# A limit of three outstanding loads on the input stream of a decay attention with gated convolution (Trainium2, one core)

## The chip, the cores and the metric

The kernel runs on one core of a Trainium2 chip (trn2). The metric is device time in microseconds (us), lower is better. The time before is a median of 216.62 us over three runs (216.39 to 217.88).

## The reference

Two stages. The first is a blocked linear attention with a decay `lam` per head: 4 batches, 8 heads, 768 positions, head size 64, in 12 blocks of 64 positions that carry a state from one block to the next. The second takes its output as x (4 x 768 x 512), makes a gate out of a causal convolution of 5 taps per channel, and two products with 512 x 512 weights.

```python
for b in range(nb):                                    # 12 blocks of 64
    qb, kb, vb = (q[:, :, sl], k[:, :, sl], v[:, :, sl])
    intra = einsum('bhij,bhjd->bhid', einsum('bhic,bhjc->bhij', qb, kb) * Dmask, vb)
    inter = einsum('bhid,bhde->bhie', qb * lam_pow, kv_state)
    out[:, :, sl] = intra + inter
    kv_state = lam_block * kv_state + einsum('bhsd,bhse->bhde', kb * rev_pow, vb)
# x = out with the heads side by side
gate = sigmoid(causal_conv5(x, conv_w))
return (gate * (x @ w_val)) @ w_out
```

## The kernel before

The work is cut into 12 steps, i = 0 to 11, one for each block of 64 positions of all batches and heads. In a step TensorE makes the scores (L469), the outer product for the state (L500), the products of scores and v (`cross` and `own`, both L535) and the part that comes from the state (`inter`, L548). The result x goes on to the convolution, whose taps run on VectorE (L659), to the product with `w_val` (`value`, L722) and, times the gate, to the product with `w_out` (`project`, L789). Both weights, and the taps, are split into a high and a low part, so that each of these products is made of three.

The order of all this is written out by hand, in the list `ORDER` (L39 to L90): 12 steps overlap, and each entry emits its instructions on its engine in turn. Every engine works through its own instructions in that order and waits where an operand isn't there; an entry that comes late holds up all behind it on the same engine.

Loads are entries of the same list. A step has one buffer `ld` (128 x 4 x 2 x 512 float32, three in rotation), filled by eight transfers of 128 x 512 (256 KB): four for q and k with the head dimension on the partitions (`ld5-q0` for step 5), two for v (`ld5-v`) and two for k with positions on the partitions (`ld5-k`). All loads and all stores of the output are issued on SyncE's queue (L333, L800), one after the other; if one has to wait, those behind it wait too. A load into a buffer waits until TensorE, ScalarE and GpSimd have read what lay there. Each transfer also carries one of eight semaphores in turn (`DMAHW0` to `DMAHW7`), and the next transfer with the same one is issued only once the former has landed: no more than eight are on their way at a time.

Who needs what: `scores` (L469) takes all four q and k pieces of its step; its first 32 products need the first two, its last 32 the other two. GpSimd scales q (L446) out of the first and third piece. `cross` needs both pieces of v, and `scale_k` (L426 on ScalarE, L430 on GpSimd) the two of k.

The lines of `land` in `plan_load` that the change touches:

```python
for part, w in where:
    nc.sync.dma_start(lds[i]["all"][:, part, w], qkv[i][:, part, w])
```

Of the kernel before, what the change touches and what calls it, by code (L numbers as in the profile page):

```python
# [31 lines left out]
H_DVE = ()  # L32
U_SPLIT = ()
T_POOL = ((5, 3),)

OVER = {"DVE": 60, "ACT": 85, "POOL": 45}

# [62 lines left out]
class Plan:  # L100
# [5 lines left out]
    def add(self, engine, ns, fn, after=(), bufs=(), lag=60, mode=0, port=False, many=0, kind=None, name=None):  # L106

        kind = kind or fn.__name__
        n = self.kinds[kind] = self.kinds.get(kind, -1) + 1
        self.names.append(name or f"{kind}{n}")  # L110
        for b in bufs:
            b.users += 1
        over = OVER.get(engine, 0)
        self.work.append(
            (engine, ns - over, fn, [a for a in after if a is not None], list(bufs), 0.0, lag + over, mode, port, many)
        )
        return len(self.work) - 1
# [20 lines left out]
def decay_attention_then_gated_conv(  # L138
# [9 lines left out]
    nc = tc.nc  # L148
# [16 lines left out]
    def buf(tag, name, shape, dt=F32):  # L165
        return work.tile(shape, dt, name=name, tag=tag, bufs=SLOTS[tag])
# [145 lines left out]
        return [t_hi, on("DVE", 1060, low, [t_hi]) if low_dve else on("POOL", 2250, low, [t_hi])]  # L312


    lds = {}
    t_ld, ld_buf = {}, {}

    def plan_load(i):
        ld_buf[i] = Buf("ld")

        def land(where, i=i):
            if i not in lds:
                t = buf("ld", "ld", [P, 4, 2, DM])
                hd = t.rearrange("q p w (a b i) -> q p w a b i", a=2, b=NB)
                lds[i] = {
                    "all": t, "qT": hd[:, 0:2, 0], "kT": hd[:, 0:2, 1], "v": hd[:, 2:4, 0], "k": hd[:, 2:4, 1],
                }
            if i == 0 and len(set(part for part, _ in where)) == 1:
                part = where[0][0]
                nc.sync.dma_start(lds[i]["all"][:, part], qkv[i][:, part])  # L330
                return
            for part, w in where:
                nc.sync.dma_start(lds[i]["all"][:, part, w], qkv[i][:, part, w])  # L333

        both = ((0,), (1,)) if i < FINE else ((0, 1),)
        for parts in both:
            where = [(part, w) for part in parts for w in range(2)]
            t = add("DMA", 1400 * len(parts), lambda where=where, land=land: land(where), [], [ld_buf[i]], lag=2300,
                name=f"ld{i}-q{parts[0]}")
            for part in parts:  # L340
                t_ld[i, part] = t
        for w, what in enumerate("vk"):
            if w == 0 or i < N - 1:
                where = [(2, w), (3, w)]
                t_ld[i, what] = add("DMA", 1400, lambda where=where, land=land: land(where), [], [ld_buf[i]], lag=2300,
                name=f"ld{i}-{what}")
# [67 lines left out]
    for i in range(N):  # L414
# [218 lines left out]
        for ct in range(NT if split or j == UNIT - 1 else 0):  # L633
            where = "PE" if (un, ct) in T_PE else "POOL" if (un, ct) in T_POOL else "DVE"
            js, width = (slice(j, j + 1), L) if split else (slice(0, UNIT), UNIT * L)
# [217 lines left out]
```

## Time and profile before

| what | value |
|---|---|
| median of three runs | 216.62 us (216.39 to 217.88) |
| the profiled execution, its own time | 218.14 us |
| its span, first to last instruction | 216.4 us |
| TensorE busy | 199.0 us, 92% of the span |
| VectorE, ScalarE, GpSimd busy | 66%, 53%, 47% |
| moved by the DMA engines | 35.70 MB, mean 165 GB/s |
| stalls of TensorE that the chain shows after 45 us | 0.30, 1.62, 1.46 and 0.71 us |

The span holds the program's instructions alone; 1.7 us of the execution's time lie outside it. The profiled execution is 1.5 us over the median of the runs. Busy time is a mean over the whole span. What a wait costs is read from the chain that ended last, at the place where it stands.

### The profile page before, as it was taken

The numbers are of one execution on the slowest core, as the hardware profiler recorded it, in microseconds if no ns is written. First come the engines' busy times: TensorE is split into PE (matmuls) and PEld (weight loads), VectorE is DVE, ScalarE is ACT, GpSimd is POOL, SyncE is SP. The second block draws the span as 40 slices with busy tenths as digits, with TensorE's granted clock in tenths as the row PEclk, the third lists the DMA queues.
The fourth block names the chain that finished last, engine by engine and source line by source line (L and its number), as shares of the span: only waits on it lengthen the run. The fifth ranks groups of instructions, "written<-read, shape, count | busy, mean of one in ns | idle before, by whom it ended". The sixth has DMA issues, their size and how long they took to land.

```text
span 216.4 us, 8533 instructions
## 1 busy us (share of the span) xinstructions
PE 199.0 (92%) x3832; PEld 175.1 (81%) x3832; DVE 143.5 (66%) x220; ACT 114.1 (53%) x193; POOL 101.6 (47%) x81
## 2 busy tenths in 40 slices
PE   8838659999997899999799998999999999999993
PEld 3437659999986698798689988899889998899983
DVE  2998998999999649725923956919448832774100
ACT  3326876886853394237437642363741239855221
POOL 1171469155999209690409175018650052655600
PEclk9976978999999999999999999999999999999999
DMA  6999999157681396734155991612141001211022
GB/s 228 352 386 387 384 353 306 53 151 245 204 286 53 101 289 252 220 123 145 37 162 164 314 301 59 177 72 100 53 138 57 5 0 55 85 60 48 3 103 91
DMA packets 19188, 35.70 MB, mean 165 GB/s; under 512 B 2384, under 2 KB 2640, under 8 KB 19152
## 3 DMA queue, kind: packets, MB, share of 16 engines
q1 hardware_dynamic: 19008, 35.16, 47.9%
q8 instruction: 30, 0.49, 1.0%
q14 instruction: 6, 0.05, 0.1%
q10 hardware_dynamic: 144, 0.00, 0.0%
HBM read 28.86 MB, written 6.29 MB: 162 GB/s over the span
## 4 chain that ended last, share of the span: by engine, by line
PE 83%; DMA 7%; DVE 6%; issue 3%; SPq 1%; ACT 0%; DVEq 0%; ACTq 0%
PE op L789 32%; PE vp L722 31%; PE xp L535 5%; PE st L500 5%; PE xp L548 5%; PE s L469 4%; DMA w_raw<-in_w_out 3%; DMA w_raw<-in_w_val 2%; DMA lam_bc<-in_lam 2%; DVE w_m L276 1%; DVE w_e L267 1%; DVE w_m L250 1%; DVE w_m L283 1%; DVE w_e L244 1%; SPq L364 1%
## 5 line engine op out<-in xcount | busy, mean ns | idle before, releaser
L659 DVE SCALAR_TENSOR_TENSOR acc<-x,conv_sb,acc 128x512 f32<-128x512 f32 x92 | 69.3, 753 | 31.4 <-ACT acc L654 29.5
L789 PE MATMUL op<-wo_hi,hs 128*128 128x512 f32 (+1 forms) x200 | 61.2, 388 | 0.3 <-issue 0.3
L722 PE MATMUL vp<-x_hi,wv_hi 128*128 128x256 f32 x192 | 55.1, 287 | 0.0
L766 POOL TENSOR_TENSOR hs<-g,hs 128x512 fp32r<-128x512 f32 x24 | 31.4, 1326 | 48.8 <-ACT hs L763 48.8
L722 PE MATMUL vp<-x_lo,wv_hi 128*128 128x256 f32 x192 | 53.7, 280 | 0.0
L722 PE MATMUL vp<-x_hi,wv_lo 128*128 128x256 f32 x192 | 53.6, 279 | 0.0
L789 PEld LDWEIGHTS op<-wo_hi,hs 128*128 128x128 f32 x200 | 35.7, 188 | 7.2
L446 POOL TENSOR_TENSOR qd<-ld,qdec 128x512 f32<-128x512 f32 x22 | 29.0, 1335 | 24.9 <-DMA ld<-in_qkv 15.9
L789 PE MATMUL op<-wo_lo,hs 128*128 128x512 f32 (+1 forms) x100 | 38.4, 384 | 0.0
L722 PEld LDWEIGHTS vp<-x_hi,wv_hi 128*128 128x128 f32 x192 | 36.5, 190 | 1.3
L722 PEld LDWEIGHTS vp<-x_lo,wv_hi 128*128 128x128 f32 x192 | 36.4, 190 | 0.3
L722 PEld LDWEIGHTS vp<-x_hi,wv_lo 128*128 128x128 f32 x192 | 36.5, 190 | 0.0
L676 ACT ACTIVATE g<-acc 128x512 f32<-128x512 f32 x23 | 13.7, 598 | 29.3 <-DVE acc L659 29.3
L735 DVE TENSOR_TENSOR g<-vp,g 128x512 f32<-128x512 f32 x24 | 16.2, 687 | 18.1 <-ACT g L676 12.4
L797 ACT COPY o<-op 128x512 f32<-128x512 f32 (+1 forms) x25 | 14.0, 569 | 25.7 <-PE op L789 19.8
L617 POOL TENSOR_TENSOR x_lo<-x,x_hi 128x1024 fp32r<-128x1024 f32 x8 | 19.9, 2493 | 11.3 <-ACT x_hi L606 8.4
L789 PEld LDWEIGHTS op<-wo_lo,hs 128*128 128x128 f32 x100 | 18.8, 188 | 4.2 <-issue 0.5
L535 PE MATMUL xp<-A,ld 64*64 64x64 f32 x768 | 17.2, 228 | 4.9 <-issue 3.1
L535 PEld LDWEIGHTS xp<-A,ld 64*64 64x64 f32 x768 | 14.4, 141 | 7.8 <-issue 4.8
L763 ACT CAST hs<-g 128x512 fp32r<-128x512 f32 x24 | 14.3, 617 | 6.7 <-DVE g L735 6.3
L500 PE MATMUL st<-ld 64*64 64x64 f32 x704 | 14.8, 236 | 3.0 <-ACT wv_hi L288 2.2
L469 PE MATMUL s<-ld 64*64 64x64 f32 x768 | 14.6, 228 | 3.2 <-DVE A L477 3.2
(56 smaller groups left out, 229.9 us busy)
## 6 DMA issues: line engine op xcount, KB each, us to landing
ld<-in_qkv SPq DMA_DIRECT2D x90, 256.0 KB, 5.3
out<-o SPq DMA_DIRECT2D x23, 256.0 KB, 2.1
w_raw<-in_w_out SPq DMA_DIRECT2D x8, 256.0 KB, 5.9
w_raw<-in_w_val SPq DMA_DIRECT2D x2, 512.0 KB, 3.9
ld<-in_qkv SPq DMA_DIRECT2D x2, 512.0 KB, 6.6
w_raw<-in_w_val SPq DMA_DIRECT2D x4, 256.0 KB, 4.8
out<-o SPq DMA_DIRECT2D x2, 128.0 KB, 1.9
conv_raw<-in_conv_w SPq DMA_DIRECT2D x1, 20.0 KB, 4.9
```

What stands on the lines that cost most here:

```text
L446: nc.gpsimd.tensor_tensor(out=s["qd"][:, p], in0=lds[i]["qT"][:, p], in1=qdec[:, :, p][:, :, None, :].to_broadcast([P, 2, NB, L]), op=ALU. ...
L469: nc.tensor.matmul(s["s", n][half(a), z, p, b], kT[half(z), p, a, b], qT[half(z), p, a, b], start=True, stop=True, skip_group_check=True,)
L500: nc.tensor.matmul(s["st"][half(z), a, p, b], k_[half(a), p, z, b], v_[half(a), p, z, b], start=True, stop=True, skip_group_check=True,)
L535: nc.tensor.matmul(s["xp"][half(p), z, a, b], lds[i]["v"][half(a), p, z, b], s["A"][half(a), z, p, b], start=t == 1 and b == 0, stop=True, ...
L617: nc.gpsimd.tensor_tensor(out=s["x_lo"].rearrange("q g b i -> q (g b) i"), in0=s["x"].rearrange("q g b i -> q (g b) i"), in1=hi.rearrange( ...
L659: nc.vector.scalar_tensor_tensor(out=to, in0=source(kk), scalar=w, in1=to, op0=ALU.mult, op1=ALU.add)
L722: nc.tensor.matmul(s["vp", u][:, f, :], w[:, ct, fs], xx[:, ct, :], start=n_mm == 0, stop=n_mm == 3 * NT - 1,)
L735: nc.vector.tensor_tensor(out=gs(u), in0=val, in1=gs(u), op=ALU.mult)
L763: nc.scalar.copy(s["h_hi"][:, us], gs(u))
L766: (nc.vector if i in H_DVE else nc.gpsimd).tensor_tensor(out=s["h_lo"][:, us], in0=gs(u), in1=s["h_hi"][:, us].bitcast(F32), op=ALU.subtract,)
L789: nc.tensor.matmul(op[:, cols], hh[:, ft, ts], w[:, ft, cols], start=n_mm == 0, stop=n_mm == 3 * NT - 1,)
L797: nc.scalar.copy(s["o", b, j][:, cols], s["op", b, j][:, cols])
```

## The change

From step 4 on, each transfer of q, k or v gets a dependency on the one three places in front of it among such transfers: SyncE issues it only when that one has landed. Stores and the loads of steps 0 to 3 and of the weights get none, and don't count among the three. `ORDER` stays, and with it each engine's list of work; the rows of TensorE, VectorE, ScalarE and GpSimd are the same as before, but for line numbers.

```diff
+CALM, AHEAD = 4, 3
...
+    late = []
+    landed = mybir.DependencyInfo(mybir.DependencyClass.Sync, mybir.DependencyReason.DATA)
...
             for part, w in where:
-                nc.sync.dma_start(lds[i]["all"][:, part, w], qkv[i][:, part, w])
+                new = nc.sync.dma_start(lds[i]["all"][:, part, w], qkv[i][:, part, w]).ins
+                if i >= CALM:
+                    if len(late) >= AHEAD:
+                        tc.add_manual_dep(new, late[-AHEAD].name, landed, reason="ahead")
+                    late.append(new)
```

The first place is SyncE's queue at step 5's and step 4's q and k. `ld_823` is the buffer of step 5, `ld_676` that of step 4; `DMAHW0` to `DMAHW7` are the eight semaphores of transfers, and the first four rows carry the numbers 0 to 3, the last four 4 to 7. Before:

```order
L333 DMA ld_823<-in_qkv 128x512 [waits PE_49,DMAHW0_49,Activation_49,Pool_49]
L333 DMA ld_823<-in_qkv 128x512 [waits DMAHW1_49]
L333 DMA ld_823<-in_qkv 128x512 [waits DMAHW2_49]
L333 DMA ld_823<-in_qkv 128x512 [waits DMAHW3_49]
L333 DMA ld_676<-in_qkv 128x512 [waits DMAHW4_49]
L333 DMA ld_676<-in_qkv 128x512 [waits DMAHW5_49]
L333 DMA ld_676<-in_qkv 128x512 [waits DMAHW6_49]
L333 DMA ld_676<-in_qkv 128x512 [waits DMAHW7_49]
```

And now, the same eight transfers:

```order
L338 DMA ld_823<-in_qkv 128x512 [waits PE_49,DMAHW0_49,Activation_49,Pool_49]
L338 DMA ld_823<-in_qkv 128x512 [waits DMAHW2_49,DMAHW1_49]
L338 DMA ld_823<-in_qkv 128x512 [waits DMAHW3_49]
L338 DMA ld_823<-in_qkv 128x512 [waits DMAHW0_49]
L338 DMA ld_676<-in_qkv 128x512 [waits DMAHW4_49,DMAHW1_49]
L338 DMA ld_676<-in_qkv 128x512 [waits DMAHW5_49,DMAHW2_49]
L338 DMA ld_676<-in_qkv 128x512 [waits DMAHW6_49,DMAHW3_49]
L338 DMA ld_676<-in_qkv 128x512 [waits DMAHW7_49,DMAHW4_49]
```

Nothing has moved, but the fourth row now waits for the first to land (`DMAHW0`), the fifth for the second, and so on to the eighth, which waits for the fifth (`DMAHW4`).

The second place is the same queue at step 9's second piece of k (first row), step 8's v (`ld_1571`), a store, and step 9's q and k (`ld_2005`). Before:

```order
L333 DMA ld_2005<-in_qkv 128x512 [waits DMAHW7_49]
L333 DMA ld_1571<-in_qkv 128x512 [waits DMAHW0_49]
L333 DMA ld_1571<-in_qkv 128x512 [waits DMAHW1_49]
L800 DMA out_0<-o_1868 128x512 [waits DMAHW2_49,Activation_49]
L333 DMA ld_2005<-in_qkv 128x512 [waits DMAHW3_49]
L333 DMA ld_2005<-in_qkv 128x512 [waits DMAHW4_49]
L333 DMA ld_2005<-in_qkv 128x512 [waits DMAHW5_49]
L333 DMA ld_2005<-in_qkv 128x512 [waits DMAHW6_49]
```

And now:

```order
L338 DMA ld_2005<-in_qkv 128x512 [waits DMAHW7_49,DMAHW4_49]
L338 DMA ld_1571<-in_qkv 128x512 [waits DMAHW5_49]
L338 DMA ld_1571<-in_qkv 128x512 [waits DMAHW6_49]
L809 DMA out_0<-o_1868 128x512 [waits Activation_49]
L338 DMA ld_2005<-in_qkv 128x512 [waits DMAHW7_49]
L338 DMA ld_2005<-in_qkv 128x512 [waits DMAHW0_49]
L338 DMA ld_2005<-in_qkv 128x512 [waits DMAHW1_49]
L338 DMA ld_2005<-in_qkv 128x512 [waits DMAHW3_49]
```

Again the order stands, and each load waits for the third load in front of it; the store is not among them, so that the first of step 9's four pieces (fifth row) waits for the first row, and the last piece for the first piece.

## Rows read from the trace of the kernel before

**Rows 1.** The page: busy us, share of the span and instructions of each engine; the granted clock of TensorE in 40 slices of 5.4 us, in tenths; and the DMA queue that carries TensorE's instructions (packets, MB, share of 16 engines).

```profile
PE 199.0 (92%) x3832; PEld 175.1 (81%) x3832; DVE 143.5 (66%) x220; ACT 114.1 (53%) x193; POOL 101.6 (47%) x81
...
PEclk9976978999999999999999999999999999999999
...
q8 instruction: 30, 0.49, 1.0%
```

**Rows 2.** The chain that ended last, in order of time: start, us, what. "issue" is time in which nothing that the profile shows was waited for.

```profile
54.47 0.93 PE s L469 x64
...
66.53 0.30 issue
...
67.46 1.09 PE xp L548 x64
68.55 0.92 PE xp L535 x61
69.47 1.62 issue
71.09 0.33 PE xp L535 x3
...
104.50 1.46 issue
...
125.38 0.93 PE s L469 x64
...
134.46 0.71 issue
```

**Rows 3.** Who waited for whom over the whole span, of SyncE's queue: us in total, times, longest.

```profile
SPq L333 <- DMA ld<-in_qkv: 7.6, 14, 1.9
```

**Rows 4.** Step 5's and step 4's q and k: line L333 alone, in four narrow windows, which hold the first, second, sixth and eighth of the eight transfers: duration of the issue in ns (min/median/max), when the issue began, and the time from issue to landing.

```profile
L333 SPq DMA_DIRECT2D ld<-in_qkv x1: 328/328/328, 44.7 to 44.7; - x1
DMA to landing us min/median/max: 3.1/3.1/3.1
...
L333 SPq DMA_DIRECT2D ld<-in_qkv x1: 433/433/433, 45.1 to 45.1; - x1
DMA to landing us min/median/max: 5.0/5.0/5.0
...
L333 SPq DMA_DIRECT2D ld<-in_qkv x1: 1800/1800/1800, 47.0 to 47.0; - x1
DMA to landing us min/median/max: 5.8/5.8/5.8
...
L333 SPq DMA_DIRECT2D ld<-in_qkv x1: 430/430/430, 49.3 to 49.3; - x1
DMA to landing us min/median/max: 4.7/4.7/4.7
```

**Rows 5.** Their reader, line L469, between 53 and 56 us: duration in ns, first and last start.

```profile
L469 PE MATMUL s<-ld x64: 218/218/219, 54.3 to 55.2; 64*64 64x64 f32 x64
```

**Rows 6.** Loads with nothing in front of them on the queue, line L333 in two windows (step 6's v, and the first piece of step 11): the same columns as rows 4.

```profile
L333 SPq DMA_DIRECT2D ld<-in_qkv x2: 420/422/425, 69.5 to 70.0; - x2
DMA to landing us min/median/max: 2.9/3.0/3.1
...
L333 SPq DMA_DIRECT2D ld<-in_qkv x1: 328/328/328, 135.7 to 135.7; - x1
DMA to landing us min/median/max: 3.5/3.5/3.5
```

**Rows 7.** DMA queues in windows: packets, MB, and the share of 16 engines' time. q1 carries loads and stores, q8 the instructions of TensorE. In turn: 46.9 to 48.4, 49.4 to 51.9, 51.9 to 53.1, 59.2 to 64.3, 64.3 to 66.8, 68.5 to 69.6 and 103.2 to 104.5 us (the window 66.83 to 68.6 has no packet of either).

```profile
q8 instruction: 1, 0.02, 6.0%
...
q1 hardware_dynamic: 470, 0.86, 100.9%
...
q8 instruction: 1, 0.02, 5.3%
...
q1 hardware_dynamic: 886, 1.60, 91.5%
...
q8 instruction: 1, 0.02, 2.5%
...
q8 instruction: 1, 0.02, 5.2%
...
q8 instruction: 1, 0.02, 5.9%
```

**Rows 8.** The second burst, line L333 in three windows: the second piece of step 9's k, then the first and the last of its four pieces of q and k; columns as in rows 4. Last, line L469 between 124.5 and 126.5 us.

```profile
L333 SPq DMA_DIRECT2D ld<-in_qkv x1: 1202/1202/1202, 114.5 to 114.5; - x1
DMA to landing us min/median/max: 5.7/5.7/5.7
...
L333 SPq DMA_DIRECT2D ld<-in_qkv x1: 432/432/432, 117.2 to 117.2; - x1
DMA to landing us min/median/max: 6.0/6.0/6.0
...
L333 SPq DMA_DIRECT2D ld<-in_qkv x1: 710/710/710, 118.7 to 118.7; - x1
DMA to landing us min/median/max: 6.4/6.4/6.4
...
L469 PE MATMUL s<-ld x64: 217/218/219, 125.2 to 126.1; 64*64 64x64 f32 x64
```

## The prediction

> **What bounds the kernel now.** I read the page first. TensorE is busy 92% of the span and nobody else over 66%; its granted clock is full (2.4 GHz) but for the first few slices [rows 1]. So only what stops TensorE counts. Next the chain that ended last: from 45 us on it is TensorE without a break but for four gaps, 0.30 us at 66.53, 1.62 at 69.47, 1.46 at 104.50 and 0.71 at 134.46, all called "issue", and none of them a wait for a load [rows 2]. Then SyncE's waits: for a landed load it waited 7.6 us in 14 pieces [rows 3], which is the limit of eight; the change will multiply this number, and that by itself costs nothing, as SyncE computes nothing. Last the single loads, to see when each lands and when its reader starts, and the DMA queues around the four gaps.
>
> The gaps. TensorE's instructions come in 30 packets on a queue of their own, 0.49 MB in all, 16 KB each [rows 1]. One occupies a DMA engine for about 1 us (2.5% of 16 engines in a window of 2.5 us) [rows 7]. Two of the gaps end a like time behind one: packet from 68.6 for 0.9 us, gap over at 71.09; packet from 103.2 for 1.2 us, gap over at 105.96; 1.5 us from its end both times [rows 2, 7]. So I take these gaps for TensorE running out of instructions. Loads bear on one of them: from 59.2 to 64.3 us the loads hold the DMA engines at 91.5% and no such packet passes; it comes once they thin out, by 64.4, and 66.83 ends the gap of 0.30 [rows 2, 7]. In front of the gaps at 69.47 and 104.50 no load was on its way; there TensorE ran through products of 64 columns (64 in 1.09 us) faster than blocks arrive [rows 2].
>
> **The change part by part.** It adds one wait to each load from the fourth late one on. It removes and moves nothing; SyncE's order stands, so a wait is passed on to every load and store behind it. Three terms touch TensorE.
>
> First term, step 4's scores. Before, the first two of the eight pieces are issued at 44.7 and 45.1 and land 3.1 and 5.0 us later, at 47.8 and 50.1; the sixth (47.0 + 5.8) lands at 52.8, the eighth (49.3 + 4.7) at 54.0 [rows 4]. The reader starts at 54.3, and its 64 products take 0.93 us on the chain, so the second half, which needs the seventh and eighth pieces, is due at 54.3 + 0.47 = 54.8 [rows 2, 5]. The eighth has 0.8 us to spare. Now the first three are issued as before. The fifth piece waits for the second, 50.1, and the eighth for the fifth. The trace has no load that follows two others at a distance; the nearest rows are loads with nothing in front, 2.9 to 3.1 us for a pair and 3.5 for another [rows 6]. Two of these in a row: 50.1 + 2 x 2.9 = 55.9 up to 50.1 + 2 x 3.5 = 57.1, against 54.8: 1.1 to 2.3 us late. TensorE does its work in order, so `value`, `project` and all behind the scores wait with it. I take 1.4, close to the pair of 2.9 to 3.1, which has a neighbour as these have. Below that it can be nothing: the second piece lands 2.3 us behind the first while an instruction packet holds one engine from 46.9 to 48.4 [rows 4, 7]; without it, at the pace of 0.63 us that the sixth to the eighth show (52.8 to 54.0 for two), it is down at 48.4, and the eighth at 54.2, in time. Above, the next instruction packet, which passed only at 51.9 when the loads had thinned (100.9% before that) [rows 7], can now come earlier and in between. The issue that met the packet of 46.9 took 1.8 us where its neighbours take 0.43 [rows 4]; 1.4 us more on the fifth piece would make the term 2.8, and I keep 2.5 as its upper end.
>
> The Trainium skill has two things to say on this term. Its page "DMA: Bandwidth & Descriptors", under "Rules for kernel authors", wants a DMA issued early and waited for late so that its fixed part overlaps other work; the change does the contrary for every third load. The same page, under "Anatomy of one DMA", gives the other path's fixed part as some 2.0 us, to which 256 KB at 436 GB/s add 0.6: an estimate of 2.6 us for a lone load, where the rows have 2.9 to 3.5. By that figure the first term would be 50.1 + 5.2 - 54.8 = 0.5, the third nothing, and the sum -0.2.
>
> Second term, the gaps at 66.5 and 69.5. With three loads queued an engine has less in front of an instruction packet, and the one of 64.4 should come some us sooner: the 0.30 goes. Of the 1.62 most stays, since its packet had no load in front of it (none in 66.83 to 68.6) and the gap at 104.50 is as long with idle DMA engines [rows 2, 7]. But that packet may be asked for sooner when the one before isn't late. Bounds 0 and -1.9 (0.30 + 1.62); I take -0.7, nearer to the row of 104.50. The gaps of 1.46 and 0.71 keep their length.
>
> The same page's section "Queues, rings and completion order" has each DMA engine take its queues in turn, a packet at a time. By that an instruction packet would never stand behind loads, the second term would be 0 and the sum +1.8. The window of 59.2 to 64.3, in which none passes, speaks against it here.
>
> Third term, step 9. The second piece of its k lands at 114.5 + 5.7 = 120.2; the first piece of q and k is issued at 117.2 and lands at 123.2, the last at 118.7 and lands at 125.1 [rows 8]. Now the first waits for 120.2 and lands at 123.1 at best, which is no later than before since the stream kept it back anyway. The last waits for that: 123.1 + 2.9 = 126.0, with 3.5 twice 127.2. Due at 125.2 + 0.47 = 125.7 [rows 8]: 0.3 to 1.5 us late. If the k piece is quicker than its 5.7 us (its issue took 1.2), nothing. I take 0.4. The store between waits behind the loads by under 1 us; ScalarE, which waits for its buffer, is busy half of the span [rows 1], and that I cost at nothing. Were that cover gone, TensorE would wait for a PSUM bank by the same under 1 us.
>
> Everything else (k and v of steps 5 to 11, and q of 6, 7, 8, 10 and 11) is asked for early enough that I cost the waits at nothing.
>
> Sum: 1.4 - 0.7 + 0.4 = +1.1 us. On the profiled execution's 218.14 that is 219.2. The profiled execution is 1.5 us over the median of the runs, and I add the same to the median: 216.62 + 1.1 = 217.7.
>
> **The rivals.** (a) The instruction packets decide, and no load is late: the second piece lands near 48.4, first and third terms are 0, and the second is between -0.3 and -1.9, say -1.3: 215.3. For it: the loads' burst at 59 to 64 us in front of a late packet. Against it: the gap at 104.50 without any load. (b) Three are too few for a burst: both step 4 and step 9 pay the upper half, because an instruction packet falls on a chain of three landings. 2.3 + 0.9 - 0.3 = +2.9: 219.5. It decides as soon as the fifth piece of the burst at 45 us lands after 53.6. For it: the 2.3 us between first and second landing, the issue of 1.8 us. Against it: the landings already came no faster than the stream. (c) The waits hide, because a load that is asked for later lands as the stream would have landed it (the first piece of step 9 does), and the instructions gain nothing: 0 +/- 0.4, 216.6. Against it: the eighth piece has only 0.8 us to spare.
>
> **How the numbers follow.** Forecast (a small loss, 216.9 to 218.6) 0.42; (a) 0.23; (b) 0.22; (c) 0.13. A measurement of this kernel tells about 1% (2.2 us) from no change: faster means under 214.5, which only (a) at its end reaches, with what I have not priced: 0.09. Slower means over 218.8: most of (b) and a little of the forecast's upper side, 0.23. The rest, 0.68, is within 1%. The range of 214.9 to 219.6 takes in (a) nearly to its end of -1.9, (c), and (b) up to its price; the forecast's own range stands above.
>
> **What would show it.** In the changed profile TensorE's chain should have a gap of 1 to 2 us inside step 4's scores, with a load as releaser, one under 1 us at step 9's, no gap at 66.5, and those of 1.46 and 0.71 unchanged; SyncE's wait for landed loads should be several times 7.6 us. A lone load should land in 2.9 to 3.5 us. The prediction is wrong if step 4's scores start on time, or if the gap of 1.62 vanishes whole.

## The result, and the profile after

The changed kernel takes 218.22 us (median of 22 runs) against 216.61 (22 runs of the kernel before, on the same chip): ratio 1.0072, 95% interval 1.0048 to 1.0096, that is 1.0 to 2.1 us slower. Here and below the medians are of all runs, while a ratio leaves out the runs that are over 1.5% above the fastest of their kernel, so that the two need not agree. The forecast was 217.7, within 1%.

The two profiles seem to say the contrary: the changed kernel's profiled execution took 216.41 us with a span of 214.6, the one of before 218.14 with 216.4. Each is one execution, and they lie at opposite ends: 216.41 is the second fastest of the 22, 218.14 is slower than all 22. So a second profile of the kernel before was taken (`e5_before_again`, below), 215.87 us with a span of 214.1. It is the nearer partner for what follows, though it too lies 0.7 us below the median of 216.61, and the changed kernel's 1.8 below its own. So the profiles show where the loss arises better than how large it is: against the second profile of before the changed one has lost 0.5 us at its end.

The page of the changed kernel, as in [rows 1]: TensorE is as busy as before, its instruction packets are the same 30.

```profile
PE 197.7 (92%) x3832; PEld 174.1 (81%) x3832; DVE 144.8 (67%) x220; ACT 113.9 (53%) x193; POOL 101.2 (47%) x81
...
PEclk9985789999999999999999999999999999999999
...
q8 instruction: 30, 0.49, 0.9%
```

SyncE's waits after, against [rows 3]: five times the time, 49 waits for 14.

```profile
SPq L338 <- DMA ld<-in_qkv: 39.0, 49, 2.4
```

The chain after, the pieces that answer to [rows 2] (start, us, what):

```profile
54.76 0.61 DVE g L744
55.37 0.04 issue
55.41 3.00 PE vp L731 x24
58.41 1.09 PE s L478 x64
...
67.09 1.09 PE xp L557 x64
68.19 0.93 PE xp L544 x64
69.12 2.96 PE op L798 x12
...
102.21 1.35 issue
...
112.14 4.22 DMA ld<-in_qkv
116.36 0.02 issue
116.38 4.14 DMA ld<-in_qkv
120.52 0.02 issue
120.53 3.18 DMA ld<-in_qkv
123.71 0.14 issue
123.84 0.69 PE s L478 x32
...
132.61 0.84 issue
```

Three things are to be seen. The gaps of 0.30 and 1.62 are gone. At 123.84 the second half of step 9's scores waits for a load, and the chain runs back from it through three landings in a row, 4.22, 4.14 and 3.18 us. And at 55.41 it is VectorE that releases TensorE, not step 4's scores: step 2's `value` waits for a PSUM bank that an `apply` of step 0 or 1 (L744) reads.

TensorE around the two scores after, in order of time (start, us, idle time before it and its releaser in brackets), first step 4's, then step 9's:

```profile
53.28 1.44 PE L478 MATMUL s<-ld 64*64 64x64 f32 x64
55.41 0.39 PE L731 MATMUL vp<-x_hi,wv_hi 128*128 128x256 f32 x1 [0.69 <-DVE g L744]
...
122.79 0.65 PE L478 MATMUL s<-ld 64*64 64x64 f32 x32
123.84 0.69 PE L478 MATMUL s<-ld 64*64 64x64 f32 x32 [0.41 <-DMA ld<-in_qkv]
```

Step 4's 64 products take 1.44 us for 1.11 without a wait: 0.33 us late, then 0.69 of waiting for VectorE, which covers it. Step 9's last 32 begin 1.05 us after the first 32; without a wait that is 0.47.

The loads behind these, line L338 in narrow windows, as in [rows 4]: the second, third and eighth of the burst of steps 5 and 4.

```profile
L338 SPq DMA_DIRECT2D ld<-in_qkv x1: 371/371/371, 43.9 to 43.9; - x1
DMA to landing us min/median/max: 3.6/3.6/3.6
...
L338 SPq DMA_DIRECT2D ld<-in_qkv x1: 1187/1187/1187, 44.3 to 44.3; - x1
DMA to landing us min/median/max: 4.0/4.0/4.0
...
L338 SPq DMA_DIRECT2D ld<-in_qkv x1: 492/492/492, 50.7 to 50.7; - x1
DMA to landing us min/median/max: 3.2/3.2/3.2
```

The second lands at 47.5 and the eighth at 53.9, where its reader is due at 53.3 + 0.47 = 53.8.

### The profile page after: what moved, and what is told of

It reads as the page before. It is cut to its first block, busy times and chain, and to the rows that moved or that the text cites. A ratio compares the mean times of both kernels' runs of the same rounds, so it can differ in the third digit from the quotient of the medians.

```text
span 214.6 us, 8535 instructions
## 1 busy us (share of the span) xinstructions
PE 197.7 (92%) x3832; PEld 174.1 (81%) x3832; DVE 144.8 (67%) x220; ACT 113.9 (53%) x193; POOL 101.2 (47%) x81
## 4 chain that ended last, share of the span: by engine, by line
PE 69%; DVE 12%; DMA 9%; issue 3%; ACT 3%; SPq 1%; POOL 1%; DVEq 0%; ACTq 0%
PE op L798 30%; PE vp L731 22%; DMA ld<-in_qkv 8%; PE xp L544 5%; PE st L509 4%; PE xp L557 4%; PE s L478 3%; DVE acc L668 2%; DVE w_m L284 2%; DMA lam_bc<-in_lam 2%; DVE w_e L268 2%; SPq L338 1%; DVE wv_lo L294 1%; DVE w_m L277 1%; ACT ld L435 1%
## 5 line engine op out<-in xcount | busy, mean ns | idle before, releaser
L775 POOL TENSOR_TENSOR hs<-g,hs 128x512 fp32r<-128x512 f32 x24 | 30.6, 1289 | 45.6 <-ACT hs L772 45.6
L685 ACT ACTIVATE g<-acc 128x512 f32<-128x512 f32 x23 | 13.8, 599 | 32.7 <-DVE acc L668 32.7
L744 DVE TENSOR_TENSOR g<-vp,g 128x512 f32<-128x512 f32 x24 | 16.2, 687 | 16.6 <-ACT g L685 10.3
L478 PEld LDWEIGHTS s<-ld 64*64 64x64 f32 x768 | 12.6, 135 | 6.6 <-DVE A L486 3.2
```

The costliest lines, as they stand in the source:

```text
L478: nc.tensor.matmul(s["s", n][half(a), z, p, b], kT[half(z), p, a, b], qT[half(z), p, a, b], start=True, stop=True, skip_group_check=True,)
L685: nc.scalar.activation(xu[un]["g"][:, at[0], js].rearrange("p u (b i) -> p b u i", b=NB), xu[un]["acc", at].rearrange("p b (u i) -> p b u ...
L744: nc.vector.tensor_tensor(out=gs(u), in0=val, in1=gs(u), op=ALU.mult)
L775: (nc.vector if i in H_DVE else nc.gpsimd).tensor_tensor(out=s["h_lo"][:, us], in0=gs(u), in1=s["h_hi"][:, us].bitcast(F32), op=ALU.subtract,)
```

## The experiments

In each of the first kernels the wait is added only to some of the loads; all late loads are still counted, so that the same load is waited for. The profiles of `e1` and `e2` aren't read, since those two executions have spans of 655 and 247 us.

**e1 and e10: the first burst alone** (q and k of steps 5 and 4).

```diff
-                    if len(late) >= AHEAD:
+                    what = "q" if part < 2 else "vk"[w]
+                    if len(late) >= AHEAD and (i, what) in ((4, "q"), (5, "q")):
```

> The limit holds for one burst alone, the eight transfers of q and k of steps 5 and 4. Theory (step 4's scores come late): +1.2 to +1.6 us over the kernel before, near 218.0, and TensorE's chain shows a gap inside step 4's scores, released by a load. Rival (the loss lies in the later bursts, or is spread): within 0.4 us of the kernel before, 216.6.

Measured: 217.59 us against 216.21, ratio 1.0041 (1.0002 to 1.0080): slower, by 0 to 1.7 us. It was run again for a profile that can be read:

> The first burst alone once more, since its first profile fell into an execution three times as long. Theory now: step 4's scores are late by 0.3 to 1 us, but TensorE then waits for VectorE's product in step 2 anyway (0.92 us in the second profile of the kernel before), so the second scores start where they do in that profile, and the time is within 0.4 us of the kernel before. Rival (my first term as forecast): +1.4 us, and the late start is seen on to the end.

Measured: 216.66 against 216.50, ratio 1.0013 (0.9987 to 1.0040). In its profile step 4's scores start a microsecond later than in the changed kernel's, and there is no wait at them or behind; step 5's start at 58.34, as after, and at 58.36 in both profiles of before:

```profile
54.37 1.11 PE L479 MATMUL s<-ld 64*64 64x64 f32 x64
55.41 0.38 PE L732 MATMUL vp<-x_hi,wv_hi 128*128 128x256 f32 x1
```

Both intervals together hold a loss of 0 to 0.9 us. The 1.4 us of my first term lies inside the first interval alone.

**e2: the second burst alone** (v of steps 4, 5 and 7, k of steps 5 and 7).

```diff
+                    if len(late) >= AHEAD and (i, what) in ((7, "v"), (4, "v"), (5, "v"), (5, "k"), (7, "k")):
```

> The limit holds for the second burst alone, v and k of steps 4, 5 and 7, which stood in front of the instruction packet of 64.4 us. Theory: 0.7 us faster than before, 215.9, up to 1.9 faster if the gaps of 0.30 and 1.62 us both go. Rival (the loss is made here, since v and k land later): 217.2 or more. Rival (instruction packets don't care about loads): 216.6, gaps as before.

Measured: 215.96 against 216.21, ratio 0.9992 (0.9960 to 1.0025). No gain that can be told from none, and no loss of 1 us either. My -0.7 lies inside the interval (-0.9 to +0.5), -1.9 doesn't.

**e3: the rest alone** (all from step 6's v on).

```diff
+                    if len(late) >= AHEAD and (i, what) not in ((4, "q"), (5, "q"), (7, "v"), (4, "v"), (5, "v"), (5, "k"), (7, "k")):
```

> The limit holds for all later loads alone, from step 6's v on. Theory: +0.4 us from step 9's scores, 217.0. Rival (loss spread over the later bursts): +1.2 us or more, 217.8. Rival (later waits hide): 216.6.

Measured: 217.97 against 216.21, ratio 1.0067 (1.0032 to 1.0102), +1.4 us (0.7 to 2.2): the size of the whole loss, and the rival's. In its profile the last 32 products of step 9's scores wait for a load:

```profile
122.43 0.65 PE L479 MATMUL s<-ld 64*64 64x64 f32 x32
123.41 0.69 PE L479 MATMUL s<-ld 64*64 64x64 f32 x32 [0.34 <-DMA ld<-in_qkv]
```

**e4: all but the first burst.**

```diff
+                    if len(late) >= AHEAD and (i, what) not in ((4, "q"), (5, "q")):
```

> The change without its first burst: q and k of steps 5 and 4 are asked for as before. Theory: 0.4 - 0.7 = -0.3 us, 216.3, so 1.4 us faster than the whole change. Rival (the first burst isn't where the loss is): 218.2 as the whole change.

Measured: 217.88 against 216.21, ratio 1.0063 (1.0028 to 1.0099). Taking the first burst out gives nothing back that can be told from none: the theory falls in its main term. Its profile shows three places, `value` of step 4, step 9's scores, and the gap behind them, which in the first profile of before was 0.71 us:

```profile
94.89 0.38 PE L732 MATMUL vp<-x_hi,wv_hi 128*128 128x256 f32 x1 [0.41 <-ACT o L807]
...
125.17 0.69 PE L479 MATMUL s<-ld 64*64 64x64 f32 x32 [0.57 <-DMA ld<-in_qkv]
...
135.56 0.45 PE L510 MATMUL st<-ld 64*64 64x64 f32 x11 [1.54 <-issue]
```

ScalarE's copy out of a PSUM bank, which `value` waits for at 94.89, had itself waited 5.44 us for a store to land:

```profile
94.25 0.59 ACT L807 COPY o<-op 128x512 f32<-128x512 f32 x1 [5.44 <-DMA out<-o]
```

That store is issued behind step 8's q. ScalarE's wait for it grows with the limit in that burst: 2.7 to 3.1 us without it and with five ahead (six profiles), 4.3 to 5.4 with three (five profiles), 9.7 with two. Of those with three ahead it reaches TensorE in `e4` alone.

**e5: the kernel before, a second profile** (no edit).

> The kernel before itself, for a second profile of it. If the gaps of 0.30 and 1.62 us after 66 us are a property of the loads in front of the instruction packets, they stand again, and the span is near 216. If they were the bad luck of the one profiled execution (1.5 us over the median of the runs), they are gone and TensorE's work after step 4's second scores ends some 2 us sooner than in the first profile.

The gaps after 66 us are gone. Of the chain (start, us, what), and TensorE at step 2's `value`:

```profile
67.00 1.09 PE xp L548 x64
68.09 0.93 PE xp L535 x64
...
102.11 1.45 issue
...
132.06 0.76 issue
```

```profile
53.30 1.11 PE L469 MATMUL s<-ld 64*64 64x64 f32 x64
55.34 0.38 PE L722 MATMUL vp<-x_hi,wv_hi 128*128 128x256 f32 x1 [0.92 <-DVE g L735]
```

From step 5's scores at 58.36 on, both profiles of before go alike but for those two places, where the first takes 2.4 us longer (the gaps of 0.30 and 1.62 us, and some more in the products around them). That is all of the difference in span, 2.3 us. And TensorE waits 0.92 us for VectorE right behind step 4's scores, which the first profile, where TensorE came a microsecond later, doesn't show.

**e6 and e7: two parts of the rest**, the loads between 114 and 132 us, and those between 69 and 102 us. Step 10's q, asked for from 104 us on between these two, and step 11's q and v, from 133 us on, are in neither.

```diff
+                    if len(late) >= AHEAD and (i, what) in ((9, "k"), (8, "v"), (9, "q"), (10, "v"), (9, "v"), (10, "k")):
```

> The limit holds for the loads between 114 and 132 us alone: step 9's k, q and v, step 8's v, step 10's v and k. Theory now (the loss of the later bursts is step 9's scores, which come 0.3 to 0.8 us late, and the gap of 0.71 us, which grows as the loads behind it last longer): +0.9 us over the kernel before, 0.5 to 1.4. Rival (the burst of steps 6 to 8 makes it): within 0.4 us of the kernel before.

```diff
+                    if len(late) >= AHEAD and (i, what) in ((6, "v"), (6, "q"), (7, "q"), (6, "k"), (8, "q"), (8, "k")):
```

> The limit holds for the loads between 69 and 102 us alone: step 6's, step 7's q, step 8's q and k. Theory: +0.3 us, by the store that is issued behind step 8's q and keeps a buffer of ScalarE's. Rival (this burst makes the loss of the later loads): +1.2 us or more.

Measured: `e6` 217.55 against 216.82, ratio 1.0010 (0.9968 to 1.0052), inconclusive between my theory and none; `e7` 216.65, ratio 0.9993 (0.9954 to 1.0033): no loss there that can be told from none or from the theory's 0.3 us. The profile of `e6` has the wait at step 9's scores, the longest with three ahead, but in a long execution (221.09 us), which was already 3 us late at step 4's scores (the window shows 29 of the 32 products):

```profile
128.34 0.65 PE L479 MATMUL s<-ld 64*64 64x64 f32 x29 [1.58 <-DMA ld<-in_qkv]
```

**e9: all but the loads between 114 and 132 us.**

```diff
+                    if len(late) >= AHEAD and (i, what) not in ((9, "k"), (8, "v"), (9, "q"), (10, "v"), (9, "v"), (10, "k")):
```

> The change without the loads between 114 and 132 us (step 9's k, q and v, step 8's v, step 10's v and k are asked for as before); all others keep the limit. Theory now (what is left of the loss is made there, at step 9's scores and the gap behind them): within 0.4 us of the kernel before, and no gap at step 9's scores. Rival (the first burst, at step 4's scores, makes it): +0.9 us or more.

Measured: 217.64 against 216.50, ratio 1.0054 (1.0021 to 1.0088). The revised theory fails here: the loads between 114 and 132 us are not all of it. In this execution step 4's scores do wait, and no wait for VectorE follows to cover it:

```profile
54.82 0.65 PE L479 MATMUL s<-ld 64*64 64x64 f32 x32
55.97 0.69 PE L479 MATMUL s<-ld 64*64 64x64 f32 x32 [0.51 <-DMA ld<-in_qkv]
56.60 0.39 PE L732 MATMUL vp<-x_hi,wv_hi 128*128 128x256 f32 x1
```

**e8 and e11: five ahead in place of three.**

```diff
-CALM, AHEAD = 4, 3
+CALM, AHEAD = 4, 5
```

> The whole change, but with five loads ahead in place of three. Theory (the loss comes from two or three latencies of some 3 us in a row): with five, a burst of eight holds one such wait, so at most a third of the loss is left, +0.5 us or less over the kernel before. Rival (any wait of SyncE on a load costs, however deep): +1.2 us or more.

> Five loads ahead once more. Theory: no difference, within 0.4 us of the kernel before. Rival (fewer loads in the queue do help the instruction packets): 0.6 us faster again.

Measured: 216.23 against 216.82, ratio 0.9969 (0.9939 to 0.9999), and 215.72 against 216.50, ratio 0.9969 (0.9942 to 0.9996). With five the loss is gone, and both times the kernel is 0.3% faster than before, by intervals that end just below 1; the rival of `e11` gave 0.6 us, measured 0.7. In its profile step 9's scores run through:

```profile
123.24 1.11 PE L478 MATMUL s<-ld 64*64 64x64 f32 x64
```

**e12: two ahead.**

```diff
-CALM, AHEAD = 4, 3
+CALM, AHEAD = 4, 2
```

> The whole change with two loads ahead in place of three. Theory (landings in a row): the eighth load of a burst now waits for three others in a row, one more than with three ahead, about 3 us later at step 4's and step 9's scores; of the first some 0.9 us is hidden behind VectorE. +4 us over the kernel before, 3 to 6, and both scores show a gap with a load as releaser. Rival (the loss isn't from landings in a row): near the +1.6 us of the whole change.

Measured: 232.95 against 216.50 by the medians, +16.5 us; the ratio is 1.0636 (1.0580 to 1.0692), +13.8 us. The direction and the two places are the theory's, the size isn't: there is a third place, and the waits are longer. TensorE's waits, both halves of step 4's scores, `value` of step 4, step 9's scores (the counts end with the windows):

```profile
55.40 0.69 PE L478 MATMUL s<-ld 64*64 64x64 f32 x32 [1.39 <-DMA ld<-in_qkv]
59.95 1.13 PE L478 MATMUL s<-ld 64*64 64x64 f32 x32 [3.86 <-DMA ld<-in_qkv]
...
105.64 0.58 PE L731 MATMUL vp<-x_hi,wv_hi 128*128 128x256 f32 x1 [4.68 <-ACT o L806]
...
141.64 0.60 PE L478 MATMUL s<-ld 64*64 64x64 f32 x23 [3.88 <-DMA ld<-in_qkv]
```

1.39 + 3.86 + 4.68 + 3.88 = 13.8 us, of 19.5 by which the span of this execution (235.42 us) exceeds that of `e5`; that the ratio gives the same 13.8 is chance. With two ahead landings in a row show at both scores, and a store stuck behind loads between them. A good part of the other 5.7 us is the clock, by the page of this profile:

```profile
PEclk9955599998599999995999997999999999999999
```

TensorE's granted clock was at its lower level (1.2 of 2.4 GHz) from 56.7 to 63.6, 104.5 to 111.3 and 142.1 to 145.5 us, each time during or right behind one of the three waits of 3.9 to 4.7 us. The 24 products of `value` behind the wait of 4.68 take 5.49 us, the next 24, at full clock, 3.02. In the other eleven profiles, whose waits are under 2 us, the clock is full from 40 us on.

What the profiles show at the three places that moved. "Wait at step 9" is the time of its 64 products over 1.11 us; "late gap" the gap near 132 to 137 us; "packet" is from the start of step 5's scores to that of the instruction packet which in the first profile of before came at 64.34.

| profile | limit | wait at step 9, us | late gap, us | packet, us |
|---|---|---|---|---|
| before, first | none | 0 | 0.71 | 5.98 |
| before, second | none | 0 | 0.76 | 3.56 |
| after | 3, all | 0.64 | 0.84 | 1.57 |
| e3 | 3, rest | 0.57 | 1.00 | 4.04 |
| e4 | 3, all but first | 0.80 | 1.54 | 2.28 |
| e6 | 3, 114 to 132 us | 1.81 | 0.99 | 3.08 |
| e7 | 3, 69 to 102 us | 0 | 0.74 | 4.04 |
| e9 | 3, not 114 to 132 us | 0.21 | 0.67 | 2.77 |
| e10 | 3, first burst | 0.17 | 0.37 | 3.21 |
| e8 | 5, all | 0 | 1.02 | 2.98 |
| e11 | 5, all | 0 | 0.42 | 3.14 |

## Why the prediction came out

The time, the side and the range held: +1.1 us forecast, +1.6 (1.0 to 2.1) measured. But that is in good part luck. Its three terms did not hold in their sizes, and errors cancelled; and both of its own signs of being wrong came: in the changed profile step 4's scores start on time (53.28 us, against 53.30 in the second profile of before), and the gap of 1.62 vanishes whole. Of the other signs the wait at step 9's scores came, no gap at 66.5, and SyncE's 39.0 us.

The first term (step 4's scores, +1.4) was the mis-sized one. The eighth piece landed 0.1 us after it was due, not 1.1 to 2.3. Two steps failed. The first is 50.1 for the second piece. Its 5.0 us go with where an instruction packet falls: in six of the twelve profiles one starts 1.0 to 2.2 us after that piece's issue, and the piece takes 4.3 to 5.0 us; in the other six it starts sooner or later, and the piece takes 3.4 to 3.9. Both profiles of before are of the first kind; after the change the packet passed at 44.2, before the data, and the piece took 3.6. I had that case as the lower end (eighth at 54.2, "in time") and took the other. The second: "TensorE does its work in order, so `value`, `project` and all behind the scores wait with it" left out that TensorE waits for VectorE right behind: 0.92 us in the second profile of before, 0.69 after. The first profile doesn't show that cover since TensorE came later there. Where the cover is short, as in `e9`, up to 0.7 us come through. The two runs with the first burst alone put it between 0 and 0.9 us. (Beside this term I wrote that the change holds back "every third load"; it holds back each load from the fourth on.)

The second term (-0.7) was read from a gap that one of the eleven profiles in the table has: the first of before, slower than all 22 runs; the two places cost 2.4 us there, more than the 1.9 that I took off the gaps. The mechanism behind it is likely, though when the packet was asked for isn't recorded: with three loads queued in that burst the packet starts 1.6 to 2.8 us after step 5's scores, without a limit in it 3.1 to 6.0. But even 5.98 us cost a gap of 0.30 at 66.5 (and with it that of 1.62), so some 5.7 are free by that profile, and in the other ten, which have no gap there, a shorter wait buys nothing; `e2` measures -0.2 (-0.9 to +0.5). The Trainium skill's page "DMA: Bandwidth & Descriptors", section "Queues, rings and completion order", has each DMA engine take turns between its queues, a packet at a time. By that an instruction packet would not stand behind loads; the table's 1.6 to 6.0 us speak against it, yet the sum by that rule, +1.8, came nearer than mine, since the gain was absent for this other reason.

The third term (step 9, +0.4) was right in its place and too small. The three landings in a row take 4.22, 4.14 and 3.18 us where I had 2.9 for the last two. In the four profiles with the limit there the last takes 3.2 to 3.5, the one before it 3.5 to 5.5; the 5.5 is in `e6`, where an instruction packet of 2.4 us falls on it. In these four the wait is 0.57 to 1.81 us, mean 0.96, against 0 to 0.21 without. Beside it I had costed two things at nothing that weren't. The late gap of 0.71 was to "keep" its length: it is 0.84 to 1.54 with the limit there, mean 1.09, and 0.37 to 1.02 without, mean 0.67; that the loads in front, which end later, lengthen it isn't shown. The store that I had priced, between step 9's loads, shows no wait of TensorE; the one behind step 8's q, which I had left among "everything else" at nothing, came through in `e4` with 0.41, with two ahead with 4.68.

By these means step 9 and the gap make (0.96 - 0.05) + (1.09 - 0.67) = 1.3 us, the size of `e3`'s +1.4 and close to the +1.6. The stretch from step 9's scores to step 10's says the same: 17.3 to 18.6 us in the four profiles, 16.3 to 17.0 in the other seven, means 17.9 and 16.6. Without `e6`, the long execution, the difference is 1.1. But `e6`, with the limit there alone, has an interval of -0.7 to +1.1, and `e9`, without it, still loses 1.2 (0.5 to 1.9), of which its profile has 0.7 at step 4's scores.

One group of loads had no run of its own: the limit on step 10's q and on step 11's q and v is in the changed kernel, `e3`, `e4` and `e9`, which lose 1.2 to 1.6 us, and in none of the other runs with three ahead. The profiles show no cost of it: step 9's first k, the next load behind step 10's q, is issued 11.0 to 11.1 us ahead of step 9's scores in all eleven, and from step 10's scores to the end all take 74.6 us.

So what is shown is that the limit of three makes landings in a row late at step 9 in all four profiles that have it there, at step 4 and at the store in some; how the 1.6 us divide among them is open.

Rival (a), that the instruction packets decide, is out: faster nowhere with three ahead. Of rival (b) the mechanism, three landings in a row that come too late, is seen at step 9, at a fraction of its price with three ahead and beyond it with two; but its own sign failed, as the fifth piece landed at 50.7 after the change and at 51.9 in `e9`, not after 53.6. Rival (c), no effect, is nearest to what five ahead does, and why the kernel is 0.3% faster there, where the packet wait is no shorter than in most profiles of before, the runs don't tell.

## What to carry to other kernels

Here a limit on outstanding transfers cost nothing until a burst needed more rounds of it than its reader had spare time. So count the rounds times the landing time of a load with neighbours, not of a lone one, and look at what else, a store above all, is queued behind the last round. Try two depths, since the cost is steep: here five gave -0.3%, three +0.7%, two +6.4%, a part of it because waits of 4 us also cost TensorE its clock. Before a gap of one profiled execution becomes a term, look where its time lies among the runs, and profile it a second time.

## What the runs showed of the hardware that was not expected

A packet with TensorE's instructions seems to hold up SyncE's issue of a load: of the first burst after, the issue at 44.3 took 1.19 us, with such a packet on its way from 44.2, where its neighbours took 0.37 and 0.33. Over the twelve profiles that can be read, 90 of SyncE's issues took over 0.8 us, and 85 of these overlap such a packet; of the 1494 shorter ones 174 do.

The "issue" gaps of TensorE go with these packets too: after 37 us the twelve profiles have 34 such gaps over 0.15 us, and each ends 1.2 to 1.6 us after the end of a packet. That bears out the prediction's reading of the gaps, though no run moved a packet to test it.

And the one packet of the table starts sooner the fewer loads are queued: 1.6 to 2.8 us with three, 3.0 and 3.1 with five, 3.1 to 6.0 with eight. The set is small, and five and eight overlap in it.
